# Two key chunks' row maxima in one VectorE instruction, through a relu on ScalarE of the chunks' difference

## The chip, the cores and the metric

The kernel runs on one core of a Trainium2 chip. The metric is device microseconds of one execution; lower is better. Engines are named as in the profile: PE is TensorE (PEld its weight loads), DVE is VectorE, ACT is ScalarE, POOL is GpSimd, SP is SyncE, which issues most of the DMAs.

## The reference, cut to what matters

Two attentions over the same 2048 tokens of width 512, with 32 heads of 16, are mixed by a gate. Side A is a full softmax attention; side B works in four segments of 512 with a causal softmax in each and a running memory between them.

```python
def _A_ref(x, wqkv, wo):
    ...
    scores = jnp.einsum("bhqd,bhkd->bhqk", q, k) * scale
    p = _softmax(scores, axis=-1)
    o = jnp.einsum("bhqk,bhkd->bhqd", p, v)
    ...
x = A_x
g = _sigmoid((x * gate_w).sum(-1, keepdims=True))
a = _A_ref(x, A_wqkv, A_wo)
b = _B_ref(x, B_wq, B_wk, B_wv, B_wo, B_beta)
return g * a + (1 - g) * b
```

The softmax subtracts the maximum of each row of scores. The change concerns only how this maximum is found on side A.

## The kernel before, in words

A first stage (to about 310 us) projects q, k and v of both sides, splits q and k into a rounded part and the rest (two float32r halves, stored in `qd` and `kd` as 32 rows per head), builds side B's memory, and takes the first maxima. The long middle (to about 1710 us) is one loop written out by hand; a short last stage finishes values and the output projection.

The middle is made of units. A unit is (side, g, c): a group g of four heads and a chunk c of 512 queries, 32 units a side. Each unit's scores are computed twice.

First for the maxima (`max_part`, lines 214 to 241). With queries on the partitions, a product over 48 rows (both halves of q and k, three of their four combinations) gives 128 queries by 512 keys in one PSUM bank (line 205, tile sm). For side A a unit has 4 heads x 4 blocks s of 128 queries x 4 key chunks kc = 64 such products, and each is reduced by one VectorE instruction to a column of `pm[:, h, s, kc]` (line 226). When the 64 are done, `finish_max` reduces the four columns to one negated maximum per query (line 183), GpSimd splits it into halves, and a transpose and a DMA put it as two more rows under the unit's q (rows 48 and 49). For side B ten products a unit are masked and reduced by an instruction that adds a mask and takes the extreme (line 238, shown as CUSTOM_DVE_ANT_0, with a second instruction that reads its accumulator).

Then for the weights (`score_part`). With keys on the partitions, a product over 50 rows (line 729, tile st) gives the score minus the maximum, and ScalarE's exponential (line 752) writes it to the tile p. A side A unit has 64 of these, a side B unit 10; each is a slot, 2368 in all, units A and B taking turns. The values product (line 786, tile ops) multiplies p by v and accumulates over a unit; at its end ScalarE copies ops away (line 790). Now and then an output product (line 898) or a later projection (line 669) uses ops in a values product's place, and is also copied out by ScalarE (lines 938, 942, 646).

Order. In iteration n of the main loop (lines 1004 to 1036) come: score product n with its exponential, then key and query loads for the maximum product m + PRE, then maximum product m = n + LEAD (LEAD = 96), so the maxima run 96 slots ahead of the scores. After every third slot (BURST = 3) follow the values of about three slots. TensorE therefore does three pairs of a score and a maximum product, which run at the same time in the two halves of its rows, then values; this is called a burst here. Score products use three banks in turn (`st_ps`), so product n needs the exponential of n - 3 to be over; maximum products use four (`banks[m % 4]`), so product m needs m - 4 to have been reduced. Every engine works through its instructions in the order in which they are written.

The list `maxs` (lines 113 to 129) fixes the order of the maximum products. For unit k of side A there are 64 of its own, and ten of side B's unit k - 1 at positions `at_` that are multiples of three: the first, `at_[0]`, six to eight places into the unit, then at distances 3, 12, 15, 24, 27, 36, 39, 48 and 51 from it. So side B's products always fall on the first slot of a burst.

Keys lie in SBUF in eight buffers for side A and two for side B (`kbuf`); `loads` issues the DMAs on SyncE in the order of first use. In the first stage `qk_tile` takes a projected tile out of PSUM (copies on ScalarE, the subtraction for the second half on VectorE) and stores it.

Of the kernel before, what the change touches and what calls it, by code (L numbers as in the profile page):

```python
# [10 lines left out]
F32 = mybir.dt.float32  # L11
F32R = mybir.dt.float32r
# [7 lines left out]
D = 512  # L20
# [19 lines left out]
NP = 6  # L40
GAP = {"A": 2, "B": 5}
LATE_T = 9
PRE = 20
NKA, NKB = 8, 2


@with_exitstack
def gated_mix(ctx, tc, x, xT, wqkv, a_wo, b_wq, b_wk, b_wv, b_wo, beta, gate_w, out):
# [8 lines left out]
    for side in "AB":  # L57
        for o in range(NO):
            for c in range(NCH):
                qd[side, o, c] = dr.tile([32, 8, CH], F32, name=f"qd{side}{o}{c}")  # L60
                kd[side, o, c] = dr.tile([32, 8, CH], F32, name=f"kd{side}{o}{c}")
    vdA = dr.tile([NG, 128, NCH, 4, 68], F32, name="vdA")
    vdB = [dr.tile([128, NG, 4, 68], F32, name=f"vdB{c}") for c in range(NCH)]
    gd = dr.tile([2, S], F32, name="gd")
# [33 lines left out]
    def unit(side, k):  # L98
        return side, k % NG, k // NG
# [11 lines left out]

    maxs = []
    for k in range(NU):
        mine = {u: iter(range(32)) for u in range(2)}
        bs = [k - 1] if 0 < k < NU - 1 else [k - 1, k] if k else []
        theirs = {r: [(unit("B", b), (r, i)) for b in bs for i in range(5)] for r in range(2)}
        start, apart = (33, (3, 3)) if k == 1 else (6, (9, 3)) if k < NU - 1 else (23, (3, 3))
        at_ = [next(m for m in range(len(maxs) + start, len(maxs) + start + 6) if m % 3 == 0)]  # L120
        while len(at_) < 10 * len(bs):
            at_.append(at_[-1] + apart[len(at_) % 2])
        for m in range(len(maxs), len(maxs) + 64 + 10 * len(bs)):
            r = (m + 1) % 2
            if m in at_ and bs:
                maxs.append(theirs[r].pop(0))
            else:
                maxs.append((unit("A", k), (r, next(mine[r]))))
        assert not theirs[0] and not theirs[1]
    last_max = {u: m for m, (u, _) in enumerate(maxs)}  # L130
    a_last = sorted(last_max["A", k % NG, k // NG] for k in range(NU))
    first_max = {u: m for m, (u, _) in reversed(list(enumerate(maxs)))}
# [4 lines left out]
    def raw(t):  # L137

        return t[:].bitcast(F32)
# [2 lines left out]

    kbuf = {"A": [kp.tile([128, 2, CH], F32R, name=f"kA{i}") for i in range(NKA)],
            "B": [kp.tile([128, 2, CH], F32R, name=f"kB{i}") for i in range(NKB)]}
    knext = {"A": 0, "B": 0}

    def load_q(u):
        side, g, c = u
# [8 lines left out]
    def load_k(u, kc):  # L157

        side, g, c = u
        t = kbuf[side][knext[side] % len(kbuf[side])]  # L160
        knext[side] += 1
        src = kd[side, g // 2, kc]
        for r in range(2):
            hs = slice(4 * (g % 2) + 2 * r, 4 * (g % 2) + 2 * r + 2)
            nc.sync.dma_start(raw(t)[64 * r:64 * r + 32], src[:, hs])
            nc.sync.dma_start(raw(t)[64 * r + 32:64 * r + 48], src[0:16, hs])
        kt_[u, kc] = t
# [36 lines left out]
    def max_product(ps, u, h, s, n0, n, k, k0=0):  # L204
        nc.tensor.matmul(ps[:, n0:n0 + n], rows(qt[u][:, :, s * 128:(s + 1) * 128], h, 48), rows(k[:, :, k0:k0 + n], h, 48),  # L205
                         start=True, stop=True)
# [3 lines left out]
    def flush_rows():  # L210
        while rows_left:
            rows_left.pop(0)()

    def max_part(m, bank):

        u, (r, i) = maxs[m]
        side, g, c = u
        if u not in pmt:
            pmt[u] = mp.tile([128, 4, 4] + [4] * (side == "A"), F32, tag="pm" + side, name="pm")
        pm = pmt[u]  # L220
        ps = bank()
        if side == "A":

            kc, s, h = i // 8, i % 8 // 2, 2 * r + i % 2
            max_product(ps, u, h, s, 0, CH, kt_[u, kc])
            nc.vector.tensor_reduce(pm[:, h, s, kc:kc + 1], ps, axis=AX.X, op=ALU.max)  # L226
            flush_rows()
        else:


            k = kt_[u, c]
            mine = [(2 * r + h, s, 128 * (s == 2) + 256 * (s == 1 and h), 128 * (s + 1))
                    for h, s in (((0, 0), (0, 2)), ((0, 1), (1, 1)), ((1, 0), (1, 2)), ((0, 3),), ((1, 3),))[i]]
            for h, s, n0, w in mine:
                max_product(ps, u, h, s, n0, w, k)
            flush_rows()
            for h, s, n0, w in mine:
                rows_left.append(lambda h=h, s=s, n0=n0, w=w: nc.vector.tensor_tensor_reduce(  # L238
                    out=tri["rest"][:, 0:w], in0=ps[:, n0:n0 + w], in1=tri["mask"][:, CH - w:], scale=-1.0, scalar=3.0e38,
                    op0=ALU.add, op1=ALU.min, accum_out=pm[:, h, s:s + 1]))  # L240
            rows_left.pop(0)()
        if m == last_max[u]:
            def finish():

                due = min(e for e in a_last if e >= last_max[u]) + LATE_T
                late.append((min(due, first[u] + LEAD - 12), u, finish_max(u)))
            todo.append((m + 1, finish))

    def run_todo(m):

        for e in [e for e in todo if e[0] <= m]:
            todo.remove(e)
            e[1]()
# [9 lines left out]
    def loads(m):  # L263

        m = min(m, len(maxs) - 1)
        while loaded[0] <= m:
            u, (r, i) = maxs[loaded[0]]
            if loaded[0] == first_max[u]:
                load_q(u)
            kc = u[2] if u[0] == "B" else i // 8  # L270
            if (u, kc) not in kt_:
                load_k(u, kc)
            loaded[0] += 1
# [3 lines left out]
    with ExitStack() as p0:  # L277
# [38 lines left out]
        def post_at(n, place, f):  # L316
            posted.setdefault((n, place), []).append(f)
# [41 lines left out]
        def xchunk(c):  # L359
            return xT[:, c * CH:(c + 1) * CH]  # L360

        def qk_tile(side, w, xc, o, dst, then=None):

            ps = pr_ps.tile([128, CH], F32, tag="pr", name="pr")
            slot(ps, lambda a, k: w[a][:, k, o * 128:(o + 1) * 128], lambda b, k: xc[b][:, k, :])
            full = wk.tile([128, CH], F32, tag="full", name="full")
            q1 = wk.tile([128, CH], F32R, tag="q1", name="q1", bufs=3)
            q2 = wk.tile([128, CH], F32R, tag="q2", name="q2", bufs=3)
            ph = {}

            def e0():
                nc.scalar.copy(full, ps)  # L372
                nc.scalar.copy(q1, full)  # L373
                nc.sync.dma_start(dst[0:16].rearrange("d h t -> (d h) t"), raw(q1))
                if then:
                    ph["mn"] = wk1.tile([128, CH], F32, tag="mn", name="mn")
                    nc.gpsimd.tensor_scalar_min(ph["mn"], full, 0.0)  # L377

            def e1():
                nc.vector.tensor_sub(q2, full, q1.bitcast(F32))  # L380
                nc.sync.dma_start(dst[16:32].rearrange("d h t -> (d h) t"), raw(q2))
                if then:
                    ph["ex"] = wk1.tile([128, CH], F32, tag="ex", name="ex")
                    nc.scalar.activation(ph["ex"], ph["mn"], AF.Exp)  # L384

            def e2():
                if then:
                    ph["ph"] = wk.tile([128, CH], F32, tag="ph", name="ph", bufs=4)
                    nc.vector.scalar_tensor_tensor(ph["ph"], full, 0.0, ph["ex"], op0=ALU.max, op1=ALU.add)
                    then(ph["ph"])  # L390
            for place, f in enumerate((e0, e1, e2)):
                post(0, place, f)
# [56 lines left out]
        def betas():  # L449
# [7 lines left out]
                nc.tensor.matmul(ps[:, NO * i:NO * i + NO], spread[:, i], beta8, start=True, stop=True)  # L457
                nc.scalar.activation(to, ps[:, NO * i:NO * i + NO], AF.Sigmoid)
            nc.vector.tensor_scalar(ogh, ogh, -1.0, 1.0, op0=ALU.mult, op1=ALU.add)
        post_at(20, 2, betas)  # L460

        def gate_logit(xg, b, col):
            jk = wk1.tile([128, D], F32, tag="mn", name="jk")
# [12 lines left out]
        for c in range(NCH):  # L476
            s0 = now[0] - (4 if c in LATER else 0)
            xn = halves(xp, "x", xchunk((c + 1) % NCH), s0 + (5 if c == 0 else 4), s0 + 8)
            if c == NCH - 1:
                wBq = halves(wp, "wq", b_wq, s0 + 7, s0 + 10)  # L480
                wBv = halves(wp, "wk", b_wv, s0 + 9, s0 + 13)
                wBk = halves(wp, "wv", b_wk, s0 + 11, s0 + 15)
            for o in range(NO if c not in LATER else 0):
                qk_tile("A", wAq, xc, o, qd["A", o, c])
            for o in range(NO):
                qk_tile("A", wAk, xc, o, kd["A", o, c])
            v_tiles("A", wAv, xc, c)
            xc = xn

# [200 lines left out]
    for (s, c), t in gate.items():  # L690
        nc.gpsimd.dma_start(t, gd["AB".index(s), c * CH:(c + 1) * CH].rearrange("(q t) -> q t", q=16)
                            .unsqueeze(0).broadcast_to([8, 16, 32]))

    tri["rest"] = dp.tile([128, CH], F32, name="rest")
    tri["mask"] = dp.tile([128, CH], F32, name="mask")
    nc.gpsimd.memset(tri["mask"], 0.0)
# [307 lines left out]
    while n < nS or queue or beside or filled[0] < len(fill):  # L1004
# [5 lines left out]
        if m < nS:  # L1010
            loads(m + PRE)

            max_part(m, lambda: banks[m % 4])
        run_todo(m)
        if n >= nS or n % (2 * BURST if n in wide else BURST) == (2 * BURST if n in wide else BURST) - 1:
            taken = 0
# [65 lines left out]
```

## Time and profile before

| | |
|---|---|
| time, median of 3 runs | 1786.01 us (1785.97 to 1787.59) |
| profiled execution, first to last instruction | 1784.1 us |
| PE busy | 1774.3 us |
| DVE busy | 1574.0 us |
| ACT busy | 1437.8 us |
| POOL busy | 641.0 us |
| mean granted TensorE clock | 0.999 |

The profiled execution's own time on the host's scale is not recorded beside its span; the median of the runs is 1.9 us above the span. Busy time is the union of an engine's instructions. A matmul's end is modelled and matmuls are pipelined, so a busy PE need not be PE at its peak. In the views quoted below, a row of groups reads: line, engine, operation, output<-inputs, shapes and count, then busy us, mean ns of one, then idle time of the engine just before them and what ended most of it. A row of the timeline reads: start, length in us, engine, line, operation, tiles and count, and in brackets idle time before it. Neighbouring instructions of one kind are merged there, so "x3" is three of them with the time from the first's start to the last's end.

### The profile page before, as it was taken

To read this page: it belongs to the slowest core of one execution; us is meant where nothing else is said; L and a number is where in the kernel's file an instruction comes from. 1 tells how busy PE (TensorE), PEld (TensorE's weight loads), DVE (VectorE), ACT (ScalarE), POOL (GpSimd) and SP (SyncE) were. 2 spreads that over 40 slices of the span, in tenths; PEclk is the share of its full clock that TensorE was granted. 3 is DMA by queue.
4 is the path that set the end of the run, shared out by engine and by line. 5 is a ranking of instruction groups with operands and counts; after the bars stand their busy time and mean duration, and the time that the engine had idled before them with its cause. 6 is when DMAs were issued, how large, how long until landed. Compare 5 with 4: busy or idle time off the path is not lost.

```text
span 1784.1 us, 40690 instructions
## 1 busy us (share of the span) xinstructions
PE 1774.3 (99%) x14945; PEld 913.3 (51%) x14945; DVE 1574.0 (88%) x3330; ACT 1437.8 (81%) x2753; POOL 641.0 (36%) x748
## 2 busy tenths in 40 slices
PE   9999999999999999999999999999999999999999
PEld 7887776444444444444444444444444444444444
DVE  4235777999999999999999999999999999999931
ACT  5455444888888888888888888888888888888884
POOL 3002222414161416443434343343434253435343
PEclk9999999999999999999999999999999999999999
DMA  6667556435463446645454545454545354544542
GB/s 222 211 222 258 190 192 191 140 97 146 107 165 108 134 121 174 152 132 135 132 139 128 146 127 145 128 145 113 154 111 154 118 141 116 147 121 136 144 162 61
DMA packets 142278, 261.55 MB, mean 147 GB/s; under 512 B 36312, under 2 KB 60408, under 8 KB 141568
## 3 DMA queue, kind: packets, MB, share of 16 engines
q1 hardware_dynamic: 140864, 257.82, 49.9%
q8 instruction: 119, 1.95, 0.5%
q0 software_dynamic: 1216, 1.14, 0.3%
q14 instruction: 79, 0.65, 0.1%
HBM read 174.39 MB, written 83.25 MB: 144 GB/s over the span
## 4 chain that ended last, share of the span: by engine, by line
PE 94%; DVE 2%; DMA 1%; ACT 1%; POOL 1%; issue 0%; SPq 0%; POOLq 0%; DVEq 0%; ACTq 0%
PE ops L786 33%; PE st L729 27%; PE sm L205 14%; PE pr L311 10%; PE ops L898 4%; PE ops L669 2%; PE sm L898 2%; POOL mn L377 1%; DMA raw<-xT 1%; PE num L499 0%; DVE pm L226 0%; DMA qdB<-q 0%; ACT ex L384 0%; DVE q L380 0%; PE mt_ps L196 0%
## 5 line engine op out<-in xcount | busy, mean ns | idle before, releaser
L752 ACT ACTIVATE p<-st 128x512 f32<-128x512 f32 x2261 | 1189.2, 600 | 152.8 <-PE sm L205 100.7
L226 DVE TENSOR_REDUCE pm<-sm 128x1 f32<-128x512 f32 x2048 | 1281.0, 683 | 11.8 <-PE sm L205 11.6
L729 PE MATMUL st<-qA,kA 50*128 50x512 f32 x2014 | 663.1, 432 | 0.0
L205 PE MATMUL sm<-kA,qA 48*128 48x512 f32 x2048 | 658.7, 428 | 0.2
L786 PE MATMUL ops<-p,vA 128*17 128x128 f32 (+3 forms) x6432 | 552.0, 441 | 0.0
L729 PEld LDWEIGHTS st<-qA,kA 50*128 50x128 f32 x2014 | 327.4, 185 | 415.2 <-ACT p L752 371.0
L205 PEld LDWEIGHTS sm<-kA,qA 48*128 48x128 f32 x2048 | 330.4, 185 | 15.6 <-issue 7.1
L848 POOL TENSOR_TENSOR rcp<-rec,minus 128x32 f32<-128x32 f32 x43 | 234.2, 5447 | 75.7 <-DMA rec<-dend 71.0
L238 DVE CUSTOM_DVE_ANT_0 rest<-sm,mask 128x128 f32<-128x128 f32 (+3 forms) x512 | 247.3, 483 | 1.9 <-PE sm L205 0.5
L786 PEld LDWEIGHTS ops<-p,vA 128*17 128x17 f32 x6432 | 130.4, 96 | 215.1 <-issue 190.1
L733 POOL TENSOR_SCALAR_AFFINE_SELECT p<-p 128x512 f32<-128x512 f32 x128 | 79.5, 637 | 324.1 <-ACT p L752 319.6
L205 PE MATMUL sm<-kB,qB 48*128 48x128 f32 (+3 forms) x512 | 166.0, 384 | 0.0
L729 PE MATMUL st<-qB,kB 50*128 50x512 f32 (+1 forms) x495 | 109.1, 329 | 0.3 <-ACT mt L199 0.3
L380 DVE TENSOR_TENSOR q<-full,q 128x512 fp32r<-128x512 f32 x56 | 38.9, 694 | 74.4 <-ACT q L373 74.4
L729 PEld LDWEIGHTS st<-qB,kB 50*128 50x128 f32 x495 | 69.8, 186 | 59.3 <-ACT p L752 48.8
L786 PE MATMUL ops<-p,vB 128*17 128x128 f32 (+3 forms) x1504 | 87.5, 350 | 0.0
L187 POOL CAST ms<-nm 128x16 fp32r<-128x16 f32 x32 | 6.7, 209 | 203.9 <-DVE nm L183 202.0
L205 PEld LDWEIGHTS sm<-kB,qB 48*128 48x128 f32 x512 | 79.9, 184 | 0.0
L377 POOL TENSOR_SCALAR mn<-full 128x512 f32<-128x512 f32 x24 | 35.7, 1489 | 101.7 <-ACT full L372 81.3
L372 ACT COPY full<-pr 128x512 f32<-128x512 f32 x56 | 32.7, 584 | 42.7 <-PE pr L311 42.4
L187 POOL CAST ms<-pm 128x16 fp32r<-128x16 f32 x32 | 6.3, 197 | 128.2 <-DVE pm L238 128.1
L864 POOL TENSOR_TENSOR v<-v,inv 128x512 f32<-128x512 f32 x31 | 39.9, 1286 | 25.7 <-DMA inv<-rdA 21.7
(188 smaller groups left out, 1628.9 us busy)
## 6 DMA issues: line engine op xcount, KB each, us to landing
kA<-kdA SPq DMA_DIRECT2D x256, 128.0 KB
vA<-vdA SPq DMA_DIRECT2D x31, 544.0 KB
kA<-kdA SPq DMA_DIRECT2D x256, 64.0 KB
kdA<-q SPq DMA_DIRECT2D x32, 256.0 KB
qdB<-q SPq DMA_DIRECT2D x32, 256.0 KB
qA<-qdA SPq DMA_DIRECT2D x64, 128.0 KB
kdB<-q SPq DMA_DIRECT2D x32, 256.0 KB
qB<-qdB SPq DMA_DIRECT2D x64, 128.0 KB
```

Source lines behind the costliest of these rows:

```text
L205: nc.tensor.matmul(ps[:, n0:n0 + n], rows(qt[u][:, :, s * 128:(s + 1) * 128], h, 48), rows(k[:, :, k0:k0 + n], h, 48), start=True, stop=True)
L226: nc.vector.tensor_reduce(pm[:, h, s, kc:kc + 1], ps, axis=AX.X, op=ALU.max)
L238: rows_left.append(lambda h=h, s=s, n0=n0, w=w: nc.vector.tensor_tensor_reduce(out=tri["rest"][:, 0:w], in0=ps[:, n0:n0 + w], in1=tri["mas ...
L311: nc.tensor.matmul(ps, l(a, k), r(b, k), start=(n == 0), stop=(n == 11))
L377: nc.gpsimd.tensor_scalar_min(ph["mn"], full, 0.0)
L729: nc.tensor.matmul(ps[:, n0:n0 + CH - q0], rows(k[:, :, b * 128:(b + 1) * 128], h, 50), rows(q[:, :, q0:], h, 50), start=True, stop=True)
L733: nc.gpsimd.affine_select(out=x, in_=x, pattern=[[0, 4], [1, 128]], base=0, channel_multiplier=-1, compare_op=ALU.is_ge, fill=0.0)
L752: nc.scalar.activation(p[:, h], ps, AF.Exp, scale=SCALE)
L786: nc.tensor.matmul(ops[32 * h:32 * h + 17, q0:q0 + 128 * w], v[:, 17 * h:17 * h + 17], p[:, h, c0:c0 + 128 * w], start=(i == 0), stop=done ...
L848: eng.tensor_tensor(r, rec, minus, op=ALU.pow)
L864: eng.tensor_mul(k["v"], k["v"], k["inv"])
L898: yield lambda i=i, x=x, w=w: nc.tensor.matmul(ps, t[:, b, x], halved[side][:, o, w], start=start and i == 0, stop=stop and i == 2)
```

## The change

For most units of side A, the rows of block s = 0 of the unit's four heads get their maxima over key chunks 0 and 1 in another way. The identity is max(a, b) = relu(a - b) + b. In the first stage the difference of the projected keys of chunk 0 and chunk 1 is formed (`apart_tile`), split in halves and stored in `dd`. In the middle a product D of q with this difference gives a - b in a bank; ScalarE's relu writes it to an SBUF tile (`over`). Four or six places later a product E of q with chunk 1 gives b, and one VectorE instruction adds the tile to the bank and takes the maximum into column 1. Column 0 of these rows is set once to -3.0e38.

"Most units" are units k = 2 to 30 of side A (`paired`), 29 of them. The D products stand at `at_[0]` + 32, 41, 50 and 59, each on the third slot of a burst. The number of products stays 64 a unit: D and E take the places of the products for chunks 0 and 1.

With it go: a buffer kD and its loads, four DMAs a unit; `pm` of side A as two fixed tiles; the keys of chunk 0 of each of the four projected tiles held in a PSUM bank until chunk 1 is projected; PRE 17 in place of 20; and a small gate computation (`betas`) at slot 25 of the first stage in place of 20.

```diff
-PRE = 20
-NKA, NKB = 8, 2
+PRE = 17
+NKA, NKB, NKD = 8, 2, 1
+PAIRED = (0,)
...
+    def paired(u):
+        return u[0] == "A" and 1 < u[1] + NG * u[2] < NU - 1
...
-        mine = {u: iter(range(32)) for u in range(2)}
+        both = paired(unit("A", k))
+        plain = {r: iter([(kc, s, h) for kc in range(NCH) for s in range(4) for h in range(2)
+                          if not both or kc > 1 or s not in PAIRED]) for r in range(2)}
+        wide_ = {r: iter([(s, h) for s in PAIRED for h in range(2)]) for r in range(2)}
+        placed = {}
...
             if m in at_ and bs:
                 maxs.append(theirs[r].pop(0))
-            else:
-                maxs.append((unit("A", k), (r, next(mine[r]))))
+                continue
+            i = placed.pop(m, None)
+            if i is None and both and m >= at_[0] + 32 and (m - at_[0] - 32) % 9 == 0 and (sh := next(wide_[r], None)):
+                i = ("D", *sh)
+                placed[m + 4 + 2 * (m + 4 in at_)] = ("E", *sh)
+            maxs.append((unit("A", k), (r, i or next(plain[r]))))
...
-            kc, s, h = i // 8, i % 8 // 2, 2 * r + i % 2
-            max_product(ps, u, h, s, 0, CH, kt_[u, kc])
-            nc.vector.tensor_reduce(pm[:, h, s, kc:kc + 1], ps, axis=AX.X, op=ALU.max)
-            flush_rows()
+            kc, s, h = i[0], i[1], 2 * r + i[2]
+            max_product(ps, u, h, s, 0, CH, kt_[u, 1 if kc == "E" else kc])
+            if kc == "D":
+                excess[u, h, s] = ex = tri["pool"].tile([128, CH], F32, tag="over", name="over")
+                nc.scalar.activation(ex, ps, AF.Relu)
+            elif kc == "E":
+                nc.vector.tensor_tensor_reduce(out=tri["rest"], in0=ps, in1=excess.pop((u, h, s)), scale=1.0, scalar=-3.0e38,
+                                               op0=ALU.add, op1=ALU.max, accum_out=pm[:, h, s, 1:2])
+                flush_rows()
+            else:
+                nc.vector.tensor_reduce(pm[:, h, s, kc:kc + 1], ps, axis=AX.X, op=ALU.max)
+                flush_rows()
...
+        def apart_tile(o, ps):
+            t = wk1.tile([128, CH], F32, tag="ex", name="apart")
+            d = [wk.tile([128, CH], F32R, tag="ph", name="apart", bufs=4) for _ in range(2)]
+            nc.vector.tensor_sub(t, kept.pop(o), ps)
+            nc.gpsimd.tensor_copy(d[0], t)
+            nc.gpsimd.tensor_sub(d[1], t, d[0].bitcast(F32))
+            for i in range(2):
+                post(2, i, lambda i=i: nc.sync.dma_start(dd[o][16 * i:16 * i + 16].rearrange("d h t -> (d h) t"), raw(d[i])))
...
-        post_at(20, 2, betas)
+        post_at(25, 2, betas)
```

More of the change, by code (lines that the diff above doesn't have):

```diff
@@ L61, in gated_mix @@
                 kd[side, o, c] = dr.tile([32, 8, CH], F32, name=f"kd{side}{o}{c}")
+    dd = [dr.tile([32, 8, CH], F32, name=f"dd{o}") for o in range(NO)]
     vdA = dr.tile([NG, 128, NCH, 4, 68], F32, name="vdA")
@@ L126, in gated_mix @@
                 maxs.append(theirs[r].pop(0))
-            else:
-                maxs.append((unit("A", k), (r, next(mine[r]))))
-        assert not theirs[0] and not theirs[1]
+                continue
[4 more added lines that the diff above has]
+            maxs.append((unit("A", k), (r, i or next(plain[r]))))
+        assert not theirs[0] and not theirs[1] and not placed
+        assert not any(next(i, None) for i in (*plain.values(), *(wide_.values() if both else ())))
     last_max = {u: m for m, (u, _) in enumerate(maxs)}
@@ L144, in gated_mix @@
             "B": [kp.tile([128, 2, CH], F32R, name=f"kB{i}") for i in range(NKB)]}
-    knext = {"A": 0, "B": 0}
+    knext = {"A": 0, "B": 0, "D": 0}
+    pmA = [mp.tile([128, 4, 4, 4], F32, name=f"pmA{i}", bufs=1) for i in range(2)]
+    excess = {}
+    owner, used = {}, [-1]
     def load_q(u):
@@ L159, in load_k @@
         side, g, c = u
+        side = "D" if kc == "D" else side
         t = kbuf[side][knext[side] % len(kbuf[side])]
+        old = owner.get((side, knext[side] - len(kbuf[side])))
+        assert not old or used[0] >= (first[old[0]] + (16 * old[1] + 15 if side == "A" else 9) if side != "D" else
+                                      max(m for m, (v, (_, i)) in enumerate(maxs) if v == old[0] and i[0] == "D") - LEAD)
+        owner[side, knext[side]] = u, kc
         knext[side] += 1
-        src = kd[side, g // 2, kc]
+        src = dd[g // 2] if kc == "D" else kd[side, g // 2, kc]
         for r in range(2):
@@ L217, in max_part @@
         side, g, c = u
-        if u not in pmt:
-            pmt[u] = mp.tile([128, 4, 4] + [4] * (side == "A"), F32, tag="pm" + side, name="pm")
+        if u not in pmt and side == "A":
+            k = g + NG * c
+            pmt[u] = pmA[k % 2]
+            if k in (2, 3):
+                for s in PAIRED:
+                    nc.vector.memset(pmt[u][:, :, s, 0], -3.0e38)
+        elif u not in pmt:
+            pmt[u] = mp.tile([128, 4, 4], F32, tag="pmB", name="pm")
         pm = pmt[u]
@@ L269, in loads @@
                 load_q(u)
-            kc = u[2] if u[0] == "B" else i // 8
+            kc = u[2] if u[0] == "B" else 1 if i[0] == "E" else i[0]
             if (u, kc) not in kt_:
@@ L360, in xchunk, with qk_tile @@
             return xT[:, c * CH:(c + 1) * CH]
-        def qk_tile(side, w, xc, o, dst, then=None):
-            ps = pr_ps.tile([128, CH], F32, tag="pr", name="pr")
+        def apart_tile(o, ps):
[6 more added lines that the diff above has]
+                post(2, i, lambda i=i: nc.sync.dma_start(dd[o][16 * i:16 * i + 16].rearrange("d h t -> (d h) t"), raw(d[i])))
+        kept = {}
+        def qk_tile(side, w, xc, o, dst, then=None, c=None):
+            if c == 0:
+                ps = kept[o] = me_sm.tile([128, CH], F32, tag="sm", name="kept")
+            else:
+                ps = pr_ps.tile([128, CH], F32, tag="pr", name="pr")
             slot(ps, lambda a, k: w[a][:, k, o * 128:(o + 1) * 128], lambda b, k: xc[b][:, k, :])
@@ L374, in e0 @@
                 nc.sync.dma_start(dst[0:16].rearrange("d h t -> (d h) t"), raw(q1))
+                if c == 1:
+                    apart_tile(o, full)
                 if then:
@@ L485, in gated_mix @@
             for o in range(NO):
-                qk_tile("A", wAk, xc, o, kd["A", o, c])
+                qk_tile("A", wAk, xc, o, kd["A", o, c], c=c)
             v_tiles("A", wAv, xc, c)
@@ L692, in gated_mix @@
                             .unsqueeze(0).broadcast_to([8, 16, 32]))
+    tri["pool"] = ctx.enter_context(tc.tile_pool(name="ov", bufs=2, reuse_waits="tile"))
+    kbuf["D"] = [dp.tile([128, 2, CH], F32R, name=f"kD{i}") for i in range(NKD)]
     tri["rest"] = dp.tile([128, CH], F32, name="rest")
@@ L1013, in gated_mix @@
             max_part(m, lambda: banks[m % 4])
+            used[0] = n
         run_todo(m)
```

## The prediction

> **What bounds the kernel now.** I read the page's head and its engine line first, then the sums by stretch, the groups by shape and the waits of the long middle, and last the timeline of one unit where the change does its work.
>
> ```profile
> span 1784.1 us, 40690 instructions
> PE 1774.3 (99%) x14945; PEld 913.3 (51%) x14945; DVE 1574.0 (88%) x3330; ACT 1437.8 (81%) x2753; POOL 641.0 (36%) x748
> ```
>
> The sums by stretch, busy time of each engine and in brackets its instructions:
>
> ```profile
> core 0: us, PE busy (x) PEld busy (x) DVE busy (x) ACT busy (x) POOL busy (x), PEclk, DMA share, GB/s
> 0.00:100.00 100.00, 96.39 (x410) 77.94 (x411) 33.36 (x55) 48.78 (x84) 14.35 (x33) 0.98 0.63 206
> ...
> 400.00:1700.00 1300.00, 1299.95 (x12177) 598.43 (x12175) 1297.96 (x2783) 1149.62 (x2227) 528.65 (x606) 1.00 0.49 135
> ```
>
> The 88% of VectorE is an average over unlike stages: in the 1300 us of the middle TensorE and VectorE are both busy to over 99.8%, and ScalarE to 88%. Two engines at 100% cannot both be the limit for long, so the busy shares do not decide; the waits do.
>
> ```profile
> L226 DVE TENSOR_REDUCE pm<-sm 128x1 f32<-128x512 f32 x1820 | 1138.3, 682 | 0.2
> L752 ACT ACTIVATE p<-st 128x512 f32<-128x512 f32 x2055 | 1080.5, 600 | 137.5 <-PE sm L205 92.6 <-PE st L729 30.3 <-POOL err L849 1.1
> L205 PEld LDWEIGHTS sm<-kA,qA 48*128 48x128 f32 x1820 | 302.2, 185 | 5.0 <-DVE pm L238 3.2
> L729 PEld LDWEIGHTS st<-qA,kA 50*128 50x128 f32 x1832 | 299.5, 185 | 380.2 <-ACT p L752 341.1 <-issue 15.6 <-ACT p L749 6.9
> ```
>
> The weight loads of the maximum products (sm), the ones that need VectorE to have emptied a bank, stood idle for VectorE 3.2 us in all of 1300. Those of the score products (st) are put down to ScalarE for 341.1 us. Much of that is only time in which values matmuls were still running, but it says where a delay would be felt. A reduce is listed at 682 ns, yet in a chain it starts sooner after its forerunner:
>
> ```profile
> 813.55 4.27 DVE L226 TENSOR_REDUCE pm<-sm 128x1 f32<-128x512 f32 x7
> 817.74 0.68 DVE L238 CUSTOM_DVE_ANT_0 rest<-sm,mask 128x512 f32<-128x512 f32 x1
> 818.35 0.08 DVE L238 DVE_READ_ACCUMULATOR2_ANT pm<- 128x1 f32 x1
> 818.35 1.28 DVE L226 TENSOR_REDUCE pm<-sm 128x1 f32<-128x512 f32 x2
> ```
>
> The same stretch on TensorE's weight loads (start, length):
>
> ```profile
> 813.40 0.18 PEld L729 LDWEIGHTS st<-qA,kA 50*128 50x128 f32 x1 [0.37 <-ACT p L752]
> 815.12 0.18 PEld L729 LDWEIGHTS st<-qA,kA 50*128 50x128 f32 x1 [0.64 <-ACT p L752]
> 816.88 0.18 PEld L729 LDWEIGHTS st<-qA,kA 50*128 50x128 f32 x1 [0.42 <-ACT p L752]
> 816.89 0.18 PEld L205 LDWEIGHTS sm<-kB,qB 48*128 48x128 f32 x1
> 817.00 0.47 PEld L729 LDWEIGHTS st<-qA,kA 50*128 50x128 f32 x2
> 817.28 0.18 PEld L205 LDWEIGHTS sm<-kA,qA 48*128 48x128 f32 x1
> 818.77 0.18 PEld L729 LDWEIGHTS st<-qA,kA 50*128 50x128 f32 x1 [0.42 <-ACT p L752]
> ```
>
> Seven reduces in 4.27 us: (4.27 - 0.68) / 6 = 0.598 us each, and the fused add-and-reduce that side B uses, 817.74 to 818.35, takes 0.61. Three slots therefore need 1.79 us of VectorE. TensorE's bursts of three slots, between the first st loads above, took 1.72, 1.76 and 1.89 us: twice below VectorE's 1.79, once above. The bursts run at TensorE's pace, and the four banks carry VectorE over the short ones. The middle is bound by TensorE together with the ScalarE exponentials that free its three score banks; VectorE is only just short of being the bound.
>
> **The change part by part.** TensorE's products are the same in number: for a pair of chunks the D product (against the keys' difference) replaces the one for one chunk, the E product stands for the other. 29 units (all of side A but the first two and the last) have four pairs, so 116 in all.
>
> VectorE loses two reduces a pair and gains one fused instruction: 2 x 0.598 - 0.61 = 0.59 us, 2.35 us a unit, 68 us in all. This is worth only what TensorE now waits for VectorE: 3.2 us by the row above. Most of it cannot go, since a unit's D slots come in its second half and VectorE has no store of finished work to carry on. Bounds: nothing, and 14.6 us (the second rival below). I take half of the visible wait, -1.6 us.
>
> ScalarE gains 116 relus over 128x512 from a bank, the shape of its exponentials. Their step, from three in 1.57 us below, is (1.57 - 0.60) / 2 = 0.485 us. A relu is issued behind the exponential of a burst's third slot (the offset of 32 from a multiple of three), so it stands ahead of the next burst's three exponentials; behind those wait the next-but-one burst's score products and, TensorE being in order, the values and all that follows. What lies free there is to be read spot by spot. The rows below are unit 12 of side A taking its maxima. The B products at 816.89 and 818.77 are at offsets 36 and 39, so the D slots (32, 41, 50, 59) are the third slots of the bursts that begin at 813.40, 818.77, 824.2 and 829.9.
>
> ```profile
> 813.57 0.59 ACT L938 COPY part<-ops 128x512 f32<-128x512 f32 x1
> 814.05 3.18 ACT L752 ACTIVATE p<-st 128x512 f32<-128x512 f32 x6
> 817.42 1.57 ACT L752 ACTIVATE p<-st 128x512 f32<-128x512 f32 x3 [0.19 <-PE sm L205]
> 818.91 0.59 ACT L790 COPY oraw<-ops 128x512 f32<-128x512 f32 x1
> 819.39 1.58 ACT L752 ACTIVATE p<-st 128x512 f32<-128x512 f32 x3
> 821.18 1.57 ACT L752 ACTIVATE p<-st 128x512 f32<-128x512 f32 x3 [0.21 <-PE sm L205]
> 823.13 3.19 ACT L752 ACTIVATE p<-st 128x512 f32<-128x512 f32 x6 [0.37 <-PE sm L205]
> 826.71 1.58 ACT L752 ACTIVATE p<-st 128x512 f32<-128x512 f32 x3 [0.40 <-PE sm L205]
> 830.47 3.26 ACT L752 ACTIVATE p<-st 128x512 f32<-128x512 f32 x6 [0.30 <-PE sm L205]
> ```
>
> ```profile
> 822.64 0.42 PEld L729 LDWEIGHTS st<-qA,kA 50*128 50x128 f32 x2
> 833.63 0.42 PEld L729 LDWEIGHTS st<-qA,kA 50*128 50x128 f32 x2
> ```
>
> First D: it falls just behind a copy of finished outputs (813.57). The six exponentials of its burst and the next take 3.18 us where 5 x 0.485 + 0.60 = 3.03 would do: 0.15 free, the relu needs 0.485, so the last of them ends 0.34 later than 817.23. The third score load of the next burst (second of the two at 817.00, so 817.28) starts 0.05 after that end. It has no reserve: 0.34 us on the path. Second D: free 0.21 + 0.115 (a step is 0.115 shorter than an exponential) = 0.33, late 0.16; the load concerned (822.87) follows its exponential's end (822.75) by 0.12, 0.07 over the 0.05: 0.09 us. Third D: 0.40 + 0.115 covers the relu: nothing, and 0.485 if that idle time were gone. Fourth D: 3.26 - 3.03 = 0.23 free, late 0.25, reserve 833.86 - 833.73 - 0.05 = 0.08: 0.17 us. Together 0.60 us a unit. The same six exponentials took 3.20 us at 494.77 and 3.19 at 1270.26:
>
> ```profile
> 494.77 3.20 ACT L752 ACTIVATE p<-st 128x512 f32<-128x512 f32 x6
> 1270.26 3.19 ACT L752 ACTIVATE p<-st 128x512 f32<-128x512 f32 x6
> ```
>
> With those the first term is 0.32 and the sum 0.58: x 29 = +16.8 us. Some is regained where a later burst would have waited for ScalarE anyway; from nothing to all of it, and I take a fifth, -3.4, since the exponentials after a late score product are late too.
>
> The Trainium skill ("ScalarE: Activation LUTs", rules for kernel authors) tells to do relu and max on VectorE, not ScalarE. By that the excess would cost VectorE one more instruction, the pair would again take two, and the change would give no time; the rows agree that ScalarE is the worse place here, for another reason, the score banks behind it.
>
> Edits I cost at nothing. In the first stage four difference tiles: one VectorE subtraction, one GpSimd copy and subtraction each, and 8 stores of 256 KB. VectorE is 33% and GpSimd 14% busy there, by the first stretch; uncovered, the stores alone would be 2.1 MB / 206 GB/s = 10 us, and I keep 2 us for the range. The difference's first operand waits in a bank of the pool that is not in use yet. SyncE issues 116 more key loads (0.42 us each, 11 MB beside 257), and all loads go out 17 slots ahead, not 20: 3 x 1.846 / 3 = 1.85 us later.
>
> ```profile
> 967.79 0.42 SPq L166 DMA_DIRECT2D kB<-kdB  x1
> 977.53 0.18 PEld L205 LDWEIGHTS sm<-kB,qB 48*128 48x128 f32 x1
> ```
>
> This last piece of a key load went out 9.7 us ahead of its use; less 1.85 and 1.7 for four more issues leaves 6.2, which I take to cover its landing (no landing of this queue is recorded). The two fills of pm and the later gate work are single small instructions under TensorE's stream.
>
> Sum: +16.8 - 3.4 - 1.6 = +11.8 us on the span of 1784.1, so 1795.9. The median of the runs shown, 1786.01, is 1.9 above that span: 1797.8, said as 1798.
>
> **The rivals.** (1) The relus are absorbed: the delay is wholly regained at bursts that wait for ScalarE anyway, and the term of 16.8 vanishes. For it: ScalarE has 150 us free in the 1300, about 0.2 a burst, and a pair comes once in three bursts, so on average 0.6 meets 0.485. Against it: at the first and fourth D the free time is 0.15 and 0.23. It gives 1786 - 1.6 = 1784.4, no change. (2) Faster: VectorE is the pace after all. Its waits can hide in the 0.08 us by which chained reduces overlap, and there are full stalls:
>
> ```profile
> L749 ACT ACTIVATE p<-st 128x512 f32<-128x512 f32 x58 | 32.6, 598 | 5.8 <-PE sm L205 3.0 <-PE st L729 2.8
> ...
> 713.77 0.19 PEld L205 LDWEIGHTS sm<-kA,qA 48*128 48x128 f32 x2 [0.32 <-DVE pm L238]
> ```
>
> Then the four D bursts, with 1.2 us of VectorE work in place of 1.79, would fall from 3 x 1300 / 2113 = 1.846 us (2055 + 58 exponentials, one a slot, in 1300 us) to the 1.72 seen above: 4 x 0.126 x 29 = 14.6 us, if the relus cost nothing: 1771.4. It decides once the hidden waits outgrow the relus' delays. Against it stand the 3.2 us and bursts already shorter than VectorE's 1.79. (3) Heavier: each relu holds the path for its whole step, as the third D would without its idle time: 116 x 0.485 = 56 us, 1842. Only a ScalarE already behind in every such burst would do that.
>
> **How the numbers follow.** Forecast 0.66, absorbed 0.17, faster 0.13, heavier 0.04. A measurement of this kernel tells about 0.2% (3.6 us) from no change. The forecast's own range is 1790 to 1806 (recovery of up to three quarters; no recovery, no relief, 2 us in the first stage). With the absorbed case taken in and the other two mostly left out the range is 1783 to 1807. Faster by over 0.2%: the faster case and a little of the absorbed, 0.14; within: most of the absorbed and the forecast's edge, 0.18; slower 0.68.
>
> **What would show it.** In the changed profile VectorE's busy time in the middle should fall by some 68 us while the span does not follow; ScalarE's busy time should rise by about 116 x 0.48 to 0.6 us; the six exponentials behind the copy should read about 3.5 us with a relu among them; bursts two after the first D should be some 0.3 us longer than now, with the wait at a score load; the first 300 us should end within 2 us of before. I am wrong if the middle's bursts get shorter, if the relu takes other than 0.6 us or its neighbours step wider, if a maximum product waits for a key load, or if the delays are found but the unit's length (45.6 us, 74 slots at 1.846 / 3) is unchanged.

## The result and the profile after

The changed kernel takes 1799.41 us (median of 4 runs, 1798.37 to 1799.9) against 1786.16 us before: a ratio of 1.007 with a 95% interval of 1.0056 to 1.0084. It is 13.25 us slower. The forecast was 1798.

The page's head of the kernel after, then its sums by stretch for the middle:

```profile
span 1796.7 us, 41229 instructions
...
PE 1785.6 (99%) x14945; PEld 915.8 (51%) x14945; DVE 1524.8 (85%) x3336; ACT 1481.7 (82%) x2869; POOL 649.5 (36%) x756
```

```profile
400.00:1700.00 1300.00, 1299.69 (x12079) 596.40 (x12078) 1235.05 (x2747) 1182.74 (x2320) 518.77 (x592) 1.00 0.53 142
```

TensorE's instructions are the same 14945 and it is still busy for all of the middle; VectorE's busy time there is 63 us less (1297.96 to 1235.05) and ScalarE's 33 more. Part of this is only that less work falls into the same 1300 us: TensorE got through 98 instructions fewer in them (12177 to 12079). Over the whole execution VectorE lost 49.2 us (1574.0 to 1524.8) and ScalarE gained 43.9 (1437.8 to 1481.7). The groups by shape of the same stretch:

```profile
L264 DVE TENSOR_REDUCE pmA<-sm 128x1 f32<-128x512 f32 x1585 | 1007.6, 683 | 34.2 <-PE sm L228 32.3 <-PE st L786 1.7
L260 DVE CUSTOM_DVE_ANT_0 rest<-sm,over 128x512 f32<-128x512 f32 x112 | 76.9, 687 | 6.1
L257 ACT ACTIVATE over<-sm 128x512 f32<-128x512 f32 x112 | 70.5, 629 | 0.0
L228 PEld LDWEIGHTS sm<-kA,qA 48*128 48x128 f32 x1695 | 283.2, 184 | 5.4 <-DVE pm L276 3.4
L786 PEld LDWEIGHTS st<-qA,kA 50*128 50x128 f32 x1812 | 298.4, 185 | 389.8 <-ACT p L809 348.8 <-issue 17.5 <-ACT p L806 6.9
```

VectorE's freed time became waiting: its reduces now stand idle 34.2 us, for TensorE. TensorE's wait for VectorE did not shrink (3.4 us against 3.2, and it is for side B's masked instruction, line 276, which the change leaves alone). Its waits for ScalarE grew from 341.1 us over 1832 score loads to 348.8 over 1812; for an equal number of loads that is 11.6 us more. The place is the one foretold: unit 12's first relu behind the copy, ScalarE's timeline and then TensorE's score loads after (the loads of the maximum products between them are left out):

```profile
818.61 0.59 ACT L995 COPY part<-ops 128x512 f32<-128x512 f32 x1
819.09 1.58 ACT L809 ACTIVATE p<-st 128x512 f32<-128x512 f32 x3
820.53 0.63 ACT L257 ACTIVATE over<-sm 128x512 f32<-128x512 f32 x1
821.01 3.10 ACT L809 ACTIVATE p<-st 128x512 f32<-128x512 f32 x6
```

```profile
821.92 0.18 PEld L786 LDWEIGHTS st<-qA,kA 50*128 50x128 f32 x1 [0.42 <-ACT p L809]
822.19 0.18 PEld L786 LDWEIGHTS st<-qA,kA 50*128 50x128 f32 x1
822.68 0.18 PEld L786 LDWEIGHTS st<-qA,kA 50*128 50x128 f32 x1 [0.30 <-ACT p L809]
...
824.11 0.18 PEld L786 LDWEIGHTS st<-qA,kA 50*128 50x128 f32 x1 [0.42 <-ACT p L809]
```

From the copy's start to the end of the third exponential behind the relu it is now 821.01 + 2 x 0.485 + 0.60 - 818.61 = 3.97 us; before, 814.05 + 3.18 - 813.57 = 3.66. The third score load waits 0.30 us for it, and the burst takes 824.11 - 821.92 = 2.19 us where it took 1.89.

The start of each maximum product's weight load after, less the same one's start before, shows where the delay grows; averaged over units 2 to 29, in us per unit:

| first slot of the burst, from the unit's first B product | growth within this burst |
|---|---|
| 0 to 35 | 0.00 |
| 36 (two bursts after the first D) | 0.28 |
| 45 (two after the second) | 0.07 |
| 54 (two after the third) | 0.00 |
| 63 (two after the fourth) | 0.07 |

The third maximum product of burst 36 has its weight load 0.37 us late in the mean, and the next burst begins 0.28 late; the difference is probably time by which that load had gone out early. The four growths are 0.42 us a unit and 12.25 us over the 29 units; the first stage ends 0.6 us later than before. Together 12.9 us, and the spans differ by 12.6.

### The profile page after: what moved, and what is told of

Read it like the earlier page. It is cut to its first block, busy times and chain, and to the rows that moved or that the text cites. A ratio compares the mean times of both kernels' runs of the same rounds, so it can differ in the third digit from the quotient of the medians.

```text
span 1796.7 us, 41229 instructions
## 1 busy us (share of the span) xinstructions
PE 1785.6 (99%) x14945; PEld 915.8 (51%) x14945; DVE 1524.8 (85%) x3336; ACT 1481.7 (82%) x2869; POOL 649.5 (36%) x756
## 5 line engine op out<-in xcount | busy, mean ns | idle before, releaser
L264 DVE TENSOR_REDUCE pmA<-sm 128x1 f32<-128x512 f32 x1816 | 1153.6, 683 | 46.8 <-PE sm L228 44.9
L786 PE MATMUL st<-qA,kA 50*128 50x512 f32 x2014 | 675.1, 435 | 0.0
L228 PE MATMUL sm<-kA,qA 48*128 48x512 f32 x1932 | 643.5, 433 | 0.4
L228 PEld LDWEIGHTS sm<-kA,qA 48*128 48x128 f32 x1932 | 313.4, 184 | 16.0 <-issue 7.1
L260 DVE CUSTOM_DVE_ANT_0 rest<-sm,over 128x512 f32<-128x512 f32 x116 | 79.7, 687 | 6.3
L257 ACT ACTIVATE over<-sm 128x512 f32<-128x512 f32 x116 | 73.0, 629 | 0.0
```

Source lines behind the costliest of these rows:

```text
L257: nc.scalar.activation(ex, ps, AF.Relu)
L260: nc.vector.tensor_tensor_reduce(out=tri["rest"], in0=ps, in1=excess.pop((u, h, s)), scale=1.0, scalar=-3.0e38, op0=ALU.add, op1=ALU.max, ...
L786: nc.tensor.matmul(ps[:, n0:n0 + CH - q0], rows(k[:, :, b * 128:(b + 1) * 128], h, 50), rows(q[:, :, q0:], h, 50), start=True, stop=True)
```

## The experiments

All times are medians, each beside runs of the kernel before on the same chip (1786.5 to 1786.8 us).

**Without the relu.** The fused instruction adds a constant tile, so the maximum leaves out chunk 0 for these rows; the D product is still made, but nobody reads it; everything else of the change stays.

```diff
-                excess[u, h, s] = ex = tri["pool"].tile([128, CH], F32, tag="over", name="over")
-                nc.scalar.activation(ex, ps, AF.Relu)
+                pass
...
-                nc.vector.tensor_tensor_reduce(out=tri["rest"], in0=ps, in1=excess.pop((u, h, s)), scale=1.0, scalar=-3.0e38,
+                nc.vector.tensor_tensor_reduce(out=tri["rest"], in0=ps, in1=tri["mask"], scale=1.0, scalar=-3.0e38,
```

> The relu is left out: the D product is still made but nothing reads it, and the fused VectorE instruction adds a constant tile in place of the excess, so the maximum leaves out chunk 0 for these rows. Loads, first stage, VectorE work and order stay those of the change. Theory (the 12.3 us in the middle are the relus' delay of the score products, and VectorE's relief is worth next to nothing): 1786 + 0.6 for the first stage, 1785 to 1788, and no shift by burst within a unit. Rival A (the time is lost to the key loads of the difference, the 17 slots of lead or the fused instruction): 1797 to 1800. Rival B (VectorE's relief is worth ten us or more and the relus cost over twenty): below 1778.

1786.82 us, ratio 1.0003 (0.9995 to 1.0012). The loss is gone, so key loads, lead, first stage and fused instruction, taken together with VectorE's relief, come to nothing. That the relief is not there hiding a cost of the others rests on the run with fewer reduces below. VectorE does keep its relief (1247.83 us busy against 1297.96):

```profile
400.00:1700.00 1300.00, 1299.71 (x12169) 598.91 (x12170) 1247.83 (x2782) 1149.15 (x2226) 528.55 (x604) 1.00 0.54 143
```

**The relu alone, on the bank.** The kernel before, and a relu of the same banks that nobody uses, written behind the reduce.

```diff
+        extra.update(at_[0] + 32 + 9 * i for i in range(4) if 1 < k < NU - 1)
...
             nc.vector.tensor_reduce(pm[:, h, s, kc:kc + 1], ps, axis=AX.X, op=ALU.max)
+            if m in extra:
+                nc.scalar.activation(tri["pool"].tile([128, CH], F32, tag="over", name="over"), ps, AF.Relu)
```

> The kernel before, with one edit: at the four slots a unit where the change has its D products, ScalarE also takes a relu of the bank into a tile that nobody reads; VectorE's reduces all stay. Theory: each unit is longer by the same 0.42 us as in the change, 29 x 0.42 = 12.2, so 1797 to 1800. Rival A: 1786. Rival B (the relief had hidden part of the relus' cost): 1805 or more.

1853.08 us, ratio 1.0372 (1.0358 to 1.0386): far above the theory. The number lies in rival B's range, but the waits of its middle show another reason than a relief that hid part of the cost:

```profile
ACT over L229 <- DVE pm L227: 43.7, 108, 0.5
```

In this program the relu waits for the reduce of the same bank, 0.40 us each in the mean, and the exponentials stand behind it. The run therefore does not tell the theories apart; it shows what a ScalarE instruction costs here once it is held up at the head of the queue: 2.27 us a unit, some 66 us over the units, 0.57 us for each of 116.

**The relu alone, on a tile.** The same, but the relu reads a constant SBUF tile and waits for nobody.

```diff
-                nc.scalar.activation(tri["pool"].tile([128, CH], F32, tag="over", name="over"), ps, AF.Relu)
+                nc.scalar.activation(tri["pool"].tile([128, CH], F32, tag="over", name="over"), tri["mask"], AF.Relu)
```

> As the relu-only run, but the extra relu at the four slots reads a constant SBUF tile, not the bank, so that neither it nor the bank waits for VectorE's reduce. Nothing else differs from the kernel before. Theory: 0.42 us a unit as in the change, 12.2 us in all, 1797 to 1800, with 0.28 us at the burst two after the first slot. Rival (the 66 us of the relu-only run were ScalarE's load, not the wait of the relu for the reduce): about 1850.

1799.24 us, ratio 1.0067 (1.0053 to 1.0081), the change's own time. The growth by burst is 0.31, 0.05, 0.00 and 0.09 us at the same four places. VectorE does all of its old work, as the third of its busy times in the middle shows, and the changed kernel is no faster than this one; rival B of the run before falls with it.

```profile
400.00:1700.00 1300.00, 1299.83 (x12076) 595.61 (x12076) 1295.29 (x2745) 1183.57 (x2319) 518.58 (x592) 1.00 0.49 134
```

**A quarter of the reduces left out.** The kernel before without the reduces of key chunk 3, which the maximum then leaves out; the products are still made.

```diff
-            nc.vector.tensor_reduce(nm, pm, axis=AX.X, op=ALU.max, negate=True)
+            nc.vector.tensor_reduce(nm, pm[:, :, :, 0:3], axis=AX.X, op=ALU.max, negate=True)
...
-            nc.vector.tensor_reduce(pm[:, h, s, kc:kc + 1], ps, axis=AX.X, op=ALU.max)
+            if kc < 3:
+                nc.vector.tensor_reduce(pm[:, h, s, kc:kc + 1], ps, axis=AX.X, op=ALU.max)
```

> The kernel before with a quarter of side A's reduces left out (those of key chunk 3, so that the maximum leaves that chunk out; the products are still made). VectorE has 16 x 0.598 = 9.6 us less to do in each unit of 45.6, four times what the change saves it. Theory (VectorE is not the bound; TensorE with the exponentials is): it can only give back the waits that TensorE's loads showed, 3.2 us, so 1781 to 1787. Rival B (VectorE at 99.9% busy sets or shares the pace): a tenth of the middle or more, below 1770.

1785.11 us, ratio 0.9993 (0.9984 to 1.0002).

```profile
400.00:1700.00 1300.00, 1300.00 (x12185) 598.64 (x12188) 1027.65 (x2329) 1150.36 (x2227) 528.57 (x604) 1.00 0.50 135
```

VectorE's busy time in the middle falls from 1297.96 to 1027.65 us, and TensorE does 12185 instructions in it where it did 12177. An engine that is busy 99.8% of a stage can lose a fifth of its work there and the stage does not get shorter.

**The D products elsewhere.** Two sets of offsets in place of 32, 41, 50, 59.

```diff
-            if i is None and both and m >= at_[0] + 32 and (m - at_[0] - 32) % 9 == 0 and (sh := next(wide_[r], None)):
+            if i is None and both and m - at_[0] in (-1, 14, 50, 53) and (sh := next(wide_[r], None)):
```

> The change with the D products at offsets -1, 14, 50 and 53 from the first B product of the unit in place of 32, 41, 50 and 59: third slots where the trace of before shows ScalarE idle for about 0.42 us or more and no copy near. Same number of relus, loads, fused instructions. Theory: the delays vanish nearly all, 1785 to 1789, and a few us less if relief at offset 14, near VectorE's only visible stalls, is worth the 3 us that they show. Rival A: 1797 to 1800 still. Rival C (each relu costs by ScalarE's total load, wherever it stands): 1797 to 1800.

1802.37 us, ratio 1.0085 (1.0071 to 1.0099): the expectation failed. The late pair (50 and 53) behaves as the spots promise: 0.02 and 0.04 us. The early pair costs 0.32 us a unit (units 2 to 29 without unit 10, of which below), all between offsets 0 and 18, for which I had added up nothing. ScalarE's timeline of the kernel before shows what I had not looked at, the bursts that follow:

```profile
795.25 1.57 ACT L752 ACTIVATE p<-st 128x512 f32<-128x512 f32 x3 [0.30 <-PE st L729]
796.99 0.26 ACT L199 CAST mt<-mt_ps 64x128 fp32r<-64x128 f32 x1 [0.16 <-PE mt_ps L196]
797.38 3.29 ACT L752 ACTIVATE p<-st 128x512 f32<-128x512 f32 x6
800.89 3.04 ACT L752 ACTIVATE p<-st 128x512 f32<-128x512 f32 x6 [0.21 <-PE sm L205]
```

After offset -1 comes the copy of the transposed maxima and then twelve exponentials with almost no free time (six of them take 3.03 us at the least). A delay that enters there is probably carried from burst to burst; this was not taken apart. Its profiled execution also fell 7.1 us behind once, in unit 10, over three bursts from 708 us on, where a maximum product waited for keys:

```profile
PE sm L228 <- DMA kA<-kdA: 3.7, 1, 3.7
```

The wait is only half of that loss. Behind it TensorE's granted clock was 0.50 from 712 to 718 us, where it was 1.00 in the rest of the middle:

```profile
712.00:718.00 6.00, 6.00 (x33) 2.68 (x33) 3.51 (x11) 2.97 (x6) 0.79 (x3) 0.50 0.78 196
```

Whether the wait brought the lower clock about, one case cannot show. Without these 7.1 us the units grow by some 11, still far from the expected nothing. With the pairs' loads earlier in the unit, loads can come late; in the change itself no such wait occurs.

```diff
-            if i is None and both and m >= at_[0] + 32 and (m - at_[0] - 32) % 9 == 0 and (sh := next(wide_[r], None)):
+            if i is None and both and m - at_[0] in (41, 50, 53, 56) and (sh := next(wide_[r], None)):
```

> The change with the D products at offsets 41, 50, 53 and 56, all behind the two copies and in the stretch where the trace of before shows ScalarE idle for 0.35 to 0.44 us a burst. Theory (the delay is the relu's 0.48 us less the idle time and reserve at its spot, and runs on where spots lie close): 0.07 + 0 + 0.04 + 0.06 = 0.17 us a unit, 5 us, 1789 to 1793. Rival C (each relu costs by ScalarE's total load, wherever it stands): 1797 to 1800.

1794.4 us, ratio 1.004 (1.0028 to 1.0053): 5 us faster than the change with the same number of relus, so it is not the total load that counts (rival C), but 1.4 us above the range. Growth by burst: 0.07 after 41, 0.01 after 50, 0.04 after 53 and 0.16 after 56, 0.28 a unit. The last, three slots behind its neighbour, cost more than I gave it.

**The copies on VectorE.** The change, with the three copies a unit out of the values bank moved from ScalarE to VectorE.

```diff
-            nc.scalar.copy(full, ops)
+            nc.vector.tensor_copy(full, ops)
...
-        return nc.vector.tensor_copy if n > wide.start + 4 else nc.scalar.copy
+        return nc.vector.tensor_copy
...
-        nc.scalar.copy(part[b], ps)
+        nc.vector.tensor_copy(part[b], ps)
```

> The change, with the copies of finished outputs out of the values bank (three a unit) on VectorE in place of ScalarE. Theory: without the copy ahead of the first D, ScalarE has 0.6 us free there in place of 0.15, the first two delays (0.35 us a unit) vanish, 1788 to 1791, unless the copy queues behind VectorE's reduces and holds back the next values by more than that. Rival (values wait for VectorE): 0.3 to 1 us at each of three copies, 1800 or more.

1833.31 us, ratio 1.026 (1.0246 to 1.0274): the rival. The growth is 0.42, 0.67 and 0.44 us at the three copies. The copy queues behind VectorE's reduces, and the next values wait for it: those of line 843 alone 22.3 us in the middle, in 28 waits of their weight loads. The relus' own first two delays are gone in this run: the growth 36 slots into the unit is 0.01 us and at 45 0.03. That fits the theory but does not show it, since a TensorE held back 0.67 us just before gives ScalarE that time as well.

**Four score banks, three for maxima.** One bank moved from the maximum products to the score products, in the change and, as a control, in the kernel before.

```diff
-        ps = banks[1 + n % BURST] if n in wide and n // BURST % 2 else st_ps.tile([128, CH], F32, tag="st", name="st")
+        ps = banks[1 + n % BURST] if n in wide and n // BURST % 2 else banks[3] if n < wide.start and n % 4 == 3 else st_ps.tile([128, CH], F32, tag="st", name="st")
...
-            max_part(m, lambda: banks[m % 4])
+            max_part(m, lambda: banks[m % 3])
```

> The change with one of the four banks of the maximum products given to the score products in the middle: four score banks, three for maxima. Theory (the relus cost time because score product n waits for the exponential of n - 3): that wait moves to n - 4, a slot further off, the 12 us vanish and some of the other waits for ScalarE too; against it VectorE with three banks can lag less, and that costs. 1770 to 1790 if the score banks are the mechanism and VectorE keeps up; over 1799 if three banks starve TensorE of maximum products.

> The kernel before with the same move of one bank, as the control. VectorE has 2.35 us a unit more to do than in the run with pairs, so with three banks its lag should hold TensorE back more: slower than that run by 5 to 60 us. If it is as fast, the pairs buy nothing even where VectorE is short of banks.

1891.98 us with pairs (ratio 1.0586, 1.0571 to 1.06) and 1877.85 us without (1.0507, 1.0493 to 1.0522). Three banks are too few for the maxima: in the control's middle the loads of the maximum products waited 45.3 us for side A's reduces, for which the kernel before shows no wait at all. That is half of what was lost; the rest was not taken apart. So these runs cannot show whether a fourth score bank would take in the relus, and that the delay acts through the three score banks rests on the order of the program and on the wait rows above. The expectation that the run with pairs would be the faster failed: it is 14 us slower, though VectorE has less to do. In its middle the maximum products' loads also waited 16.1 us for the relus to empty their bank (line 257, 63 waits), beside 42.2 us for the reduces; that is of the size of the 14 us, and was not tested further.

## Why the prediction was right

**What bounds the kernel.** Right, and shown twice: VectorE's relief alone gives nothing (1786.82), nor does four times as much (1785.11). The argument from two of three bursts shorter than VectorE's 1.79 us, and from the small idle time of the maximum products' loads, was the one that held; the 99.8% busy share was not.

**Relief for VectorE, taken at -1.6 us.** Too much; without the relu the middle gained nothing that shows, and what TensorE still waits for is side B's instruction. The lower bound, nothing, was the answer.

**The relus' delay, 0.58 us a unit and 16.8 us in all, less 3.4 regained.** The mechanism was right: the run with the relu of a tile has the change's time with VectorE's old work. By spots: 0.32 was forecast for the first and 0.28 came; 0.09 and 0.07 for the second; nothing and nothing for the third; 0.17 and 0.07 for the fourth. The fourth was the one mis-sized. The fifth that I took off as regained was not seen to be regained anywhere, since no burst gets shorter by more than 0.01 us after a delay. Sum: 12.25 measured in the units, 11.8 forecast for the whole. That the two lie so close is in part luck: the spots were 16.8 - 12.25 = 4.6 us too dear, and the two deductions that the runs do not bear out, 3.4 and 1.6, make up for it.

**The signs.** The six exponentials behind the copy with the relu among them, 819.09 to 822.58, take 3.49 us (about 3.5 was foretold), and the burst two after that D is 0.30 us longer (some 0.3). The busy times moved the way foretold but by less: VectorE's by 49.2 us over the whole execution where 68 was said, ScalarE's by 43.9 where 56 to 70 was said. For ScalarE an estimate from the prediction's rows fits: a relu that fills the gap before an exponential adds its step of 0.485 and takes away the 0.115 by which chained instructions overlap, and 116 x 0.37 is 43 us. This was not tested.

**Edits costed at nothing.** The first stage ends 0.6 us later in the profiled execution of the change and 1.0 us earlier in that without the relu. Such differences mean little: with the relu of a tile, which edits nothing there, it ended 1.9 us later, and the granted clock between 9 and 16 us was 0.51 in that execution and 0.76 in that of the kernel before. No maximum product of the change waited for keys, as the row of the 9.7 us lead suggested; the moved set shows that the margin is not large.

**The rivals.** "Absorbed" fell: nothing was regained. "Faster" fell with the reduces left out. "Heavier" did not come about in the change. The relu that waited for a reduce cost as much as that, 66 us, but through its own wait of 0.40 us and not through a ScalarE that was already behind. The upper end of the forecast's own range, 1806, is by its own terms (1786 + 16.8 + 2) 1804.8; nothing hangs on it. That ScalarE is the worse place for the relu than VectorE, as the prediction says, no run shows: none put the relu on VectorE.

## What to carry to other kernels

A busy share near 100% names a candidate for the bound, not the bound: look at who waits for it, and whether its consumer's steps are ever shorter than its own work for them; leaving out part of its work is a cheap test. Work moved to an engine with a free 12% costs by the place where it lands: read that engine's idle time in the very burst, the reserve of what is queued behind it, and the bursts after that. What was left of the delay after that idle time and reserve reached TensorE here, and was not made good later.

## What the runs showed of the hardware

A relu from a bank took 629 ns in the mean (line 257, above) where the exponentials of the same shape took 600 before and 611 in the same kernel, but they follow each other in as close a sequence: between 400 and 1700 us of the kernel after, the steps from an exponential's start to a relu's and from a relu's to an exponential's have a median of 477 ns where ScalarE did not idle, as between exponentials. In such a chain the length of an instruction overstates what it takes from its engine; the step is what delays the next.
